# Loading each K or V unit by two 64-partition transfers (even and odd partitions) instead of one

## The chip, the cores and the metric

The kernel runs on one core of one Trainium2 chip. The metric is the device time of one execution in microseconds (us), the median of several. "Unit" is one 512 KB block of the K or V cache, the amount that the kernel loads and consumes at a time.

## The reference

Two rounds of attention over a KV cache (one new token, batch 4, 32 query heads on 8 KV heads, 8192 positions, head size 128) and a gated feed-forward block, each with a layer norm and a residual:

```python
q = (x @ wq).reshape(B, Sq, Hq, Dh) ...            # B=4, Sq=1, D=512, Hq=32, Dh=128
k = jnp.repeat(k_cache, rep, axis=1)               # k_cache, v_cache: (4, 8, 8192, 128) bf16
scores = jnp.einsum("bhqd,bhkd->bhqk", q, k) * (Dh ** -0.5)
o = jnp.einsum("bhqk,bhkd->bhqd", _softmax(scores), v)
...
x = x + A(layernorm(x)); x = x + B(layernorm(x))   # and both once more, same weights and caches
```

Each cache is 67 MB. The kernel keeps 11 of the 32 V units of a batch on chip between the two rounds, so 468 units are loaded: 256 of K and 212 of V, 245 MB, and 14 MB of weights.

## The kernel before

A unit is 2048 cache rows of 256 bytes. Partition p takes rows 16p to 16p+15, a contiguous run of 4 KB. Seven ring slots hold the units in flight; SyncE issues each load as soon as PE has released the slot. `T.dma` adds the waits that are needed and records what the next reader has to wait for.

```python
CR = 2048; NB = CR // P          # P = 128, NB = 16 rows in a partition
NRING = 7
...
def pump():
    while lptr[0] < len(loads):
        kind, x, sm = loads[lptr[0]]
        if kind == "w":                        # a weight piece of 0.9 or 1 MB, every fifth load at first
            T.dma("sp", x[0], x[1], sm, writes=[x[2]])
        else:
            ap, key = home[x]                  # ring slot or kept slot, [128, 2048] bf16
            if not released.get(key, True):
                return
            ...
            src = cache[b, g, c * CR:(c + 1) * CR, :].rearrange("(p t) d -> p (t d)", p=P)
            T.dma("sp", ap, src, sm, writes=[key])
        lptr[0] += 1
```

PE transposes a K unit (16 matmuls), multiplies the transposed unit with the queries, and later multiplies V units with the softmax weights (16 matmuls a unit).

## Time and profile before

698.9 us (median of 3; 697 to 700 us in groups of runs). What matters:

| | before |
|---|---|
| bytes moved by the load queue | 259.3 MB |
| rate in steady stretches | 403 to 409 GB/s |
| transfer time of a unit at 406 GB/s | 1.29 us |
| 468 units and 13.9 MB of weights at that rate | 638 of 700 us |
| one issue on SyncE | 0.33 us |

These lines are from the page of the kernel before: all packets; the load queue with its packets, MB and share of 16 engines' time; the chain of waits that ended last, by engine and by line; the K transposes on PE (count, busy us, mean ns, idle us ahead of them and what ended most of it); and the K loads (count, size, us from issue to landing).

```profile
DMA packets 75117, 260.93 MB, mean 373 GB/s; under 512 B 7672, under 2 KB 13568, under 8 KB 74496
q1 hardware_dynamic: 75008, 259.30, 96.1%
...
PE 51%; DMA 37%; issue 5%; DVE 4%; ACT 2%; SPq 1%; ACTq 0%
...
L408 PE MATMUL ps<-ident,ring 128*128 128x128 bf16 x4096 | 294.6, 230 | 36.8 <-DMA ring<-in_A_k_cache_dram 35.0
...
ring<-in_A_k_cache_dram SPq DMA_DIRECT2D x256, 512.0 KB, 7.6
```

The transfer engines are taken 96% of the time. A K load needs 7.6 us from issue to landing although its own share of the stream is 1.29 us: by these two numbers about five others stand before it.

The windows view of four steady stretches of the kernel before (window and its length in us; busy us of PE, weight load, DVE, ACT and POOL, with counts; granted clock; share of the DMA engines; GB/s):

```profile
100.00:150.00 50.00, 44.83 (x771) 35.14 (x772) 21.54 (x35) 20.03 (x24) 0.00 (x0) 0.88 1.02 403
205.00:245.00 40.00, 38.04 (x618) 29.14 (x615) 25.98 (x46) 22.68 (x29) 0.00 (x0) 0.95 1.02 406
360.00:400.00 40.00, 36.16 (x584) 26.78 (x581) 23.09 (x40) 20.27 (x26) 0.00 (x0) 0.98 1.03 409
520.00:560.00 40.00, 35.99 (x594) 27.08 (x591) 23.41 (x39) 21.38 (x27) 0.00 (x0) 0.98 1.03 409
```

SyncE's own waits in the kernel before (what released it: total us, times, longest us):

```profile
SPq L62 <- PE ps L408: 263.9, 225, 11.8
SPq L62 <- PE ps L507: 157.9, 111, 8.3
```

Its K issues, by source line (count: shortest, median, longest ns; first and last start us):

```profile
L92 SPq DMA_DIRECT2D ring<-in_A_k_cache_dram x256: 327/328/6203, 1.6 to 645.4; - x128
```

And a piece of its timeline (start us, length us; the view joins SyncE's issues of one kind that follow one another, over its pauses too, and counts them behind the x; the eight that take 8.70 us are 0.33 us each, so 6.1 us of that are pauses):

```profile
204.89 1.24 SPq L92 DMA_DIRECT2D ring<-in_A_k_cache_dram  x2
207.13 0.33 SPq L92 DMA_DIRECT2D ring<-in_A_v_cache_dram  x1
208.47 8.70 SPq L92 DMA_DIRECT2D ring<-in_A_k_cache_dram  x8
218.17 0.33 SPq L92 DMA_DIRECT2D ring<-in_A_v_cache_dram  x1
```

### The profile page before, as it was taken

How to read it: one execution, taken by the hardware profiler on the slowest of the kernel's cores; microseconds unless marked ns; L12 is line 12 of the kernel's file. 1: busy time of each engine (PE TensorE's matmuls, PEld its weight loads, DVE VectorE, ACT ScalarE, POOL GpSimd, SP SyncE). 2: the span in 40 equal slices, each digit the busy share in tenths (PEclk: the TensorE clock that was granted, in tenths of full speed). 3: DMA queues.
4: the chain of work that ended last, by engine and by line, in shares of the span. 5: the costliest groups of instructions: out<-in, count | busy, mean ns of one | idle time of the engine just before them, and what ended most of it. 6: DMA issues, size and time to landing. Idle time of an engine off the chain costs nothing.

```text
span 699.7 us, 25539 instructions
## 1 busy us (share of the span) xinstructions
PE 584.9 (84%) x11552; PEld 479.2 (68%) x11552; DVE 298.8 (43%) x635; ACT 235.1 (34%) x296; POOL 0.7 (0%) x6
## 2 busy tenths in 40 slices
PE   3977879878699899987799898988799876799876
PEld 2755657657677687766677677767777675777665
DVE  1544524443156645452165534543155510266501
ACT  1533324331056434420154434432055500055400
POOL 0000000000000000000000000000000000000000
PEclk9999879995589889985599879995589955599855
DMA  8999999999889999999999999999899989999992
GB/s 349 388 388 408 385 395 407 401 401 409 328 284 411 404 399 407 406 408 392 335 343 409 402 370 385 370 409 407 320 382 409 408 325 410 349 338 361 343 396 75
DMA packets 75117, 260.93 MB, mean 373 GB/s; under 512 B 7672, under 2 KB 13568, under 8 KB 74496
## 3 DMA queue, kind: packets, MB, share of 16 engines
q1 hardware_dynamic: 75008, 259.30, 96.1%
q8 instruction: 90, 1.47, 0.9%
q14 instruction: 19, 0.16, 0.1%
HBM read 259.26 MB, written 0.00 MB: 371 GB/s over the span
## 4 chain that ended last, share of the span: by engine, by line
PE 51%; DMA 37%; issue 5%; DVE 4%; ACT 2%; SPq 1%; ACTq 0%
DMA ring<-in_A_k_cache_dram 27%; PE ps L408 25%; PE ps L507 9%; DMA ring<-in_A_v_cache_dram 8%; PE ps L424 7%; PE ps L572 3%; PE ps L596 2%; DMA wq_sb<-in_A_wq_dram 2%; PE ps L531 1%; SPq L92 1%; PE ps L632 1%; PE ps L548 1%; ACT ktp L248 1%; PE ps L479 1%; DVE negm L436 1%
## 5 line engine op out<-in xcount | busy, mean ns | idle before, releaser
L408 PE MATMUL ps<-ident,ring 128*128 128x128 bf16 x4096 | 294.6, 230 | 36.8 <-DMA ring<-in_A_k_cache_dram 35.0
L408 PEld LDWEIGHTS ps<-ident,ring 128*128 128x128 bf16 x4096 | 251.4, 103 | 79.0 <-DMA ring<-in_A_k_cache_dram 54.1
L246 DVE COPY ktp<-ps 128x1024 bf16<-128x1024 bf16 x320 | 215.6, 689 | 206.3 <-PE ps L408 205.4
L248 ACT ACTIVATE ktp<-ps 128x1024 bf16<-128x1024 bf16 x192 | 195.5, 1023 | 259.7 <-PE ps L408 259.7
L424 PE MATMUL ps<-ktp,qpad 128*32 128x512 bf16 x1024 | 111.3, 401 | 3.3 <-ACT ktp L248 2.6
L507 PE MATMUL ps<-pp,ring 128*128 128x4 bf16 x2688 | 88.9, 166 | 22.5 <-issue 13.1
L507 PEld LDWEIGHTS ps<-pp,ring 128*128 128x128 bf16 x2688 | 82.5, 102 | 35.5 <-issue 21.8
L424 PEld LDWEIGHTS ps<-ktp,qpad 128*32 128x32 bf16 x1024 | 27.7, 93 | 37.7 <-ACT ktp L248 7.5
L507 PE MATMUL ps<-pp,kept 128*128 128x4 bf16 x1408 | 45.8, 166 | 8.7 <-DMA kept<-in_A_v_cache_dram 6.3
L507 PEld LDWEIGHTS ps<-pp,kept 128*128 128x128 bf16 x1408 | 41.4, 101 | 16.6 <-DMA kept<-in_A_v_cache_dram 7.9
L564 ACT ACTIVATE lnv<-var,eps_sb 128x4 f32<-128x4 f32 x10 | 3.0, 297 | 142.9 <-DVE var L551 142.9
L515 DVE TENSOR_TENSOR oT<-ps,invL 128x4 bf16<-128x4 f32 x64 | 10.6, 166 | 79.8 <-PE ps L507 79.7
L438 ACT ACTIVATE pp<-ps,negm 128x512 bf16<-128x512 f32 x32 | 22.0, 687 | 26.7 <-DVE negm L436 22.7
L572 PE MATMUL ps<-xnT,wq_sb 128*128 128x4 bf16 x640 | 18.7, 166 | 11.5 <-DMA wq_sb<-in_A_wq_dram 7.7
L436 DVE TENSOR_REDUCE negm<-ps 128x1 f32<-128x512 f32 x32 | 22.1, 690 | 11.6 <-PE ps L424 10.0
L572 PEld LDWEIGHTS ps<-xnT,wq_sb 128*128 128x128 bf16 x640 | 17.9, 104 | 12.0 <-DMA wq_sb<-in_A_wq_dram 7.8
L531 PE MATMUL ps<-oT,wo_sb 128*128 128x4 bf16 x640 | 21.3, 166 | 5.5 <-DVE oT L515 2.9
L531 PEld LDWEIGHTS ps<-oT,wo_sb 128*128 128x128 bf16 x640 | 20.0, 104 | 7.8 <-issue 4.7
L479 PE MATMUL ps<-ident,pp 128*128 128x128 bf16 x128 | 14.5, 303 | 1.3 <-DVE pp L469 1.0
L551 DVE TENSOR_REDUCE var<-ps 128x4 f32<-128x16 f32 x10 | 1.7, 175 | 28.2 <-PE ps L548 28.2
L479 PEld LDWEIGHTS ps<-ident,pp 128*128 128x128 bf16 x128 | 12.4, 140 | 1.9 <-DVE pp L469 1.7
L248 ACT ACTIVATE pp<-ps 128x1024 bf16<-128x1024 bf16 x6 | 6.1, 1025 | 16.8 <-PE ps L479 16.8
(66 smaller groups left out, 158.1 us busy)
## 6 DMA issues: line engine op xcount, KB each, us to landing
ring<-in_A_k_cache_dram SPq DMA_DIRECT2D x256, 512.0 KB, 7.6
ring<-in_A_v_cache_dram SPq DMA_DIRECT2D x168, 512.0 KB, 7.6
kept<-in_A_v_cache_dram SPq DMA_DIRECT2D x44, 512.0 KB, 12.2
wq_sb<-in_A_wq_dram SPq DMA_DIRECT2D x1, 4096.0 KB, 12.4
wo_sb<-in_A_wo_dram SPq DMA_DIRECT2D x4, 1024.0 KB, 11.6
wg_sb<-in_B_w_gate_dram SPq DMA_DIRECT2D x2, 896.0 KB, 12.0
wu_sb<-in_B_w_up_dram SPq DMA_DIRECT2D x2, 896.0 KB, 11.9
wd_sb<-in_B_w_down_dram SPq DMA_DIRECT2D x2, 896.0 KB, 9.2
```

The costliest lines, as they stand in the source:

```text
L246: T.op("dve", lambda e: e.tensor_copy(dst, src), reads=reads, writes=writes)
L248: T.op("act", lambda e: e.activation(dst, src, ACTF.Copy), reads=reads, writes=writes)
L408: T.op("pe", lambda e: e.matmul(stg[:, t * P:(t + 1) * P], lhsT=ap[:, blk * Dh:(blk + 1) * Dh], rhs=ident[:], is_transpose=True, start=Tru ...
L424: T.op("pe", lambda e: e.matmul(ps[32 * j:32 * (j + 1), bk * BW:(bk + 1) * BW], lhsT=qp, rhs=ktp[:, s, (j % 2) * 512:(j % 2 + 1) * 512], s ...
L436: T.op("dve", lambda e: e.tensor_reduce(negm[:, q, c:c + 1], bank(bk), AX.X, ALU.max, negate=True), reads=[f"pb{bk}"], writes=[f"negm{q}_{ ...
L438: T.op("act", lambda e: e.activation(pp[:, q, c * 512:(c + 1) * 512], bank(bk), ACTF.Exp, bias=negm[:, q, c:c + 1], scale=1.0, accum_out=l ...
L479: T.op("pe", lambda e: e.matmul(stg[:, t * P:(t + 1) * P], lhsT=pp[:, q, blk * P:(blk + 1) * P], rhs=ident[:], is_transpose=True, start=Tr ...
L507: T.op("pe", lambda e: e.matmul(ps[:, bk * BW:bk * BW + REP], lhsT=ap[:, (NM * j + m) * Dh:(NM * j + m + 1) * Dh], rhs=pp[:, q, col:col + ...
L515: T.op("dve", lambda e: e.tensor_tensor(oT[:, l, g * REP:(g + 1) * REP, b], ps[:, bk * BW:bk * BW + REP], invL[:, q, g * REP:(g + 1) * REP ...
L531: T.op("pe", lambda e: e.matmul(ps[:, OPJ * BW + nq * B:OPJ * BW + (nq + 1) * B], lhsT=wo_sb[:, h, nq * P:(nq + 1) * P], rhs=oT[:, l, h, : ...
L572: T.op("pe", lambda e: e.matmul(misc[:, h * B:(h + 1) * B], lhsT=wq_sb[:, kt, h * Dh:(h + 1) * Dh], rhs=xnT[:, kt * B:(kt + 1) * B], start ...
L596: T.op("pe", lambda e: e.matmul(ps[:, bk * BW + fo * B:bk * BW + (fo + 1) * B], lhsT=w_sb[:, kt, fo * P:(fo + 1) * P], rhs=xnT[:, kt * B:( ...
```

## The change

Each unit is loaded by two transfers of 256 KB, one into the even and one into the odd partitions. Bytes, runs (4 KB), slots and the place of every row stay the same; the reader waits for both.

```diff
+    NSPL = 2
...
-                    src = cache[b, g, c * CR:(c + 1) * CR, :].rearrange("(p t) d -> p (t d)", p=P)
-                    T.dma("sp", ap, src, sm, writes=[key])
+                    src = cache[b, g, c * CR:(c + 1) * CR, :].rearrange("(p i t) d -> i p (t d)", i=NSPL, t=NB)
+                    for i in range(NSPL):
+                        T.dma("sp", ap[bass.ds(i, P // NSPL, step=NSPL), :], src[i], sm, writes=[key] if i == 0 else [])
+                    T.res[key].w = (sm, T.semval[id(sm)])
```

The intent can only be a better spread or finer grain of the transfers; nothing is taken away.

## The prediction

> **What bounds the kernel now.** The transfers. The page's queue part gives the one queue 96.1% of the 16 DMA engines' span, for 259 MB. By windows, steady stretches (100 to 175, 205 to 330, 355 to 400 us) move 400 to 415 GB/s at a DMA share of about 1.0. At 406 GB/s a 512 KB unit takes 1.29 us; 468 units are 604 us and 13.9 MB of weights 34 us: 638 of 700 us. The rest is at the four block boundaries (near 190, 350, 500, 565 us, 164 to 250 GB/s) and the two ends. PE is busy 84% but follows: in the chain of waits K transfers hold 27%, V transfers 8%. SyncE issues a load when PE has let a slot go (264 and 158 us of its waits), with about 6 of 7 ring slots in flight.
>
> The packet records agree: 59904 packets of 4 KB, median 159 ns, 629.8 us summed over 16 engines; 7672 semaphore packets of 4 bytes, 9.3 ns each.
>
> **What the change does.** Same bytes, same 4 KB packets, same slots and waits. A unit becomes two transfers of 64 partitions (every other one): 468 more transfers.
> - Removed: nothing. The unit's wait is for both.
> - SyncE: an issue is busy 0.33 us; two in a row start 0.37 to 0.43 us apart. Some 0.8 us a unit is under 1.29 us: off the critical path.
> - Engines: one more semaphore packet per engine and unit, 9.3 ns; the first data packet behind one often takes 165 to 172 instead of 159 ns, so 9 to 16 ns each, 4.4 to 7.5 us for 468. About 90% of the span is transfer-bound: 4 to 7 us show.
>
> **The doubtful term: which engine writes which partitions.** [...] only 4 to 7 us are lost: about 704 us. [...] No trace here shows which; I give the first a little over one half. The engines are not in step now (a transfer's 16 landings spread over 2.4 us, median)[...].
>
> **Prediction.** 712 us, between the two; range 698 to 940. Faster by over 2%: 0.03; within 2%: 0.51; slower: 0.46.
>
> **What would show it.** Queue part: about 7490 more packets, all tiny, same MB. If 4 KB packets stay at 159 to 163 ns and steady stretches at 395 to 410 GB/s, the first reading holds: 700 to 710 us. [...] If instead the share falls and SyncE's issues run back to back, issuing limits.
>
> **What would make it wrong.** [...] a costlier transfer boundary than 16 ns; rows 8 KB apart reading slower from HBM than neighbours; a queue that fills sooner with 10 packets per engine and unit instead of 9 (issues blocked up to 6.2 us already occur).

The forecast of 712 us lies between two cases: 704 us, the first reading, which is the kernel before and 4 to 7 us for the boundaries, and a much slower one, which also sets the upper end of the range, 940 us.

## More of the kernel before

The order of rows within a unit does not matter as long as K and V share it; some experiments use that.

SyncE waits 422 of 700 us for PE to release a slot.

SPq, which is SyncE issuing transfers, has 1% of the chain.

## The result, and the profile after

730.2 us (median of 4, 727.4 to 732.7) against 698.8 us: ratio 1.0445, 95% interval 1.038 to 1.051. A ratio here is the mean time of one kernel's fast runs over that of the other's of the same rounds, so not quite the ratio of the medians. The result is correct and 4.5% slower. The time lay inside the range, but the forecast of 712 us had 13 of the 31 us that were lost.

The same lines of the page of the kernel after:

```profile
DMA packets 82609, 260.99 MB, mean 360 GB/s; under 512 B 15160, under 2 KB 21056, under 8 KB 81984
q1 hardware_dynamic: 82496, 259.33, 95.8%
...
PE 39%; DMA 27%; SPq 23%; issue 6%; DVE 3%; ACT 2%; ACTq 0%
...
L411 PE MATMUL ps<-ident,ring 128*128 128x128 bf16 x4096 | 298.3, 231 | 50.7 <-DMA ring<-in_A_k_cache_dram 49.1
...
ring<-in_A_k_cache_dram SPq DMA_DIRECT2D x512, 256.0 KB, 5.4
```

The packets grew by 7488, all of them tiny, as expected. SPq went from 1% to 23% of the chain. A load now lands 5.4 us after its issue instead of 7.6: the queue ahead of it has become shorter, although the kernel is slower. Where SyncE needs longer for a unit in the runs below, it is the same: over all loads the median from issue to landing is 7.7 us before, 5.2 us after, 5.8 us in e5, and 2.6 us in e2, with transfers of 128 KB.

The same four windows:

```profile
100.00:150.00 50.00, 41.30 (x724) 32.41 (x724) 20.14 (x33) 18.57 (x22) 0.00 (x0) 0.88 1.02 391
205.00:245.00 40.00, 37.08 (x576) 27.47 (x572) 24.21 (x37) 22.80 (x26) 0.00 (x0) 1.00 1.01 369
360.00:400.00 40.00, 37.42 (x588) 28.69 (x585) 22.23 (x34) 20.04 (x25) 0.00 (x0) 0.95 0.99 370
520.00:560.00 40.00, 34.16 (x510) 26.45 (x507) 18.95 (x29) 17.93 (x20) 0.00 (x0) 0.88 1.01 378
```

The rate fell from 403 to 409 GB/s to 369 to 391, while the DMA share still reads about 1.0. The share adds up the times of packets, and these grew: the 4 KB packets take 647.8 us of each engine instead of 629.8. In the records of single packets, the median of the 4 KB packets is 159 ns before and after, and those of at most 160 ns even rose from 67 to 88% of all; but those over 250 ns rose from 1.9 to 3.5% (36.6 to 69.0 us of each engine). That these include waiting is the author's reading, not shown. A share of 0.99 to 1.02, as here at 369 to 391 GB/s, is no proof that the engines are the limit.

SyncE in the kernel after, in the same three views, its waits first:

```profile
SPq L62 <- PE ps L411: 37.4, 44, 8.5
...
SPq L62 <- PE ps L510: 15.5, 15, 4.8
```

Its K issues:

```profile
L92 SPq DMA_DIRECT2D ring<-in_A_k_cache_dram x512: 471/596/2760, 1.6 to 670.4; - x171
```

And its timeline from 226 to 236 us:

```profile
226.10 10.16 SPq L92 DMA_DIRECT2D ring<-in_A_k_cache_dram  x15
```

SyncE's waits for PE went from 422 to 53 us. The 15 issues of this timeline take 10.16 us; in their single records the pauses are 0.04 us between the halves of a unit and about 0.10 us around the wait, so SyncE issues nearly without a pause. One issue of 64 partitions takes 0.47 us after a pause and 0.54 to 0.60 us back to back, against 0.33 us (0.38 back to back) for 128 partitions. The shortest cycle of a unit is 0.54 + 0.04 + 0.60 us and about 0.10 us around the wait: 1.28 us, the same as the 1.29 us that the transfers need. In addition 83 of the 936 issues took over 0.75 us (81 in the repeat e14). Had they taken 0.57 us like the others, the mean below would be about 1.27 us (an estimate from these records): it is they that lift it over 1.29. The packet records tell what they go with: 81 of the 83 overlap one of the 90 packets of 16 KB of the page's instruction queue (q8), and 73 end 0.35 to 0.40 us after the end of such a packet, as none of the other 853 issues does. Meeting a packet is not enough: in e5, below, 77 short issues overlap one, and only 5 of 468 issues are long. Why issues hang there is not shown. To have one number for all runs: SyncE's own time per unit is the time from its first to its last cache issue, less its waits for PE and the weight issues, divided by 468. It is 0.54 us before (where 54 of the 468 issues took over 0.75 us, up to 6.2) and (706.8 - 52.9 - 6.3) / 468 = 1.38 us after.

Theory 1: SyncE's issuing limits the changed kernel. Theory 2, the rival: the 468 additional transfer boundaries cost the 16 engines, 31 us / 468 = 67 ns each.

### The profile page after: what moved, and what is told of

The parts are those of the page before. It is cut to its first block, busy times and chain, and to the rows that moved or that the text cites. A ratio compares the mean times of both kernels' runs of the same rounds, so it can differ in the third digit from the quotient of the medians.

```text
span 725.5 us, 26007 instructions
## 1 busy us (share of the span) xinstructions
PE 592.1 (82%) x11552; PEld 483.5 (67%) x11552; DVE 299.5 (41%) x635; ACT 235.1 (32%) x296; POOL 0.7 (0%) x6
## 4 chain that ended last, share of the span: by engine, by line
PE 39%; DMA 27%; SPq 23%; issue 6%; DVE 3%; ACT 2%; ACTq 0%
SPq L92 23%; PE ps L411 20%; DMA ring<-in_A_k_cache_dram 19%; DMA ring<-in_A_v_cache_dram 6%; PE ps L427 5%; PE ps L510 5%; PE ps L575 2%; DMA wq_sb<-in_A_wq_dram 2%; PE ps L599 2%; ACT ktp L249 1%; PE ps L534 1%; DVE negm L439 1%; PE ps L635 1%; PE ps L551 1%; DMA kept<-in_A_v_cache_dram 1%
## 5 line engine op out<-in xcount | busy, mean ns | idle before, releaser
L411 PE MATMUL ps<-ident,ring 128*128 128x128 bf16 x4096 | 298.3, 231 | 50.7 <-DMA ring<-in_A_k_cache_dram 49.1
L411 PEld LDWEIGHTS ps<-ident,ring 128*128 128x128 bf16 x4096 | 254.8, 104 | 93.9 <-DMA ring<-in_A_k_cache_dram 67.3
L510 PE MATMUL ps<-pp,ring 128*128 128x4 bf16 x2688 | 90.6, 166 | 28.8 <-DMA ring<-in_A_v_cache_dram 15.9
```

Of the source, the lines that this page charges most:

```text
L411: T.op("pe", lambda e: e.matmul(stg[:, t * P:(t + 1) * P], lhsT=ap[:, blk * Dh:(blk + 1) * Dh], rhs=ident[:], is_transpose=True, start=Tru ...
L510: T.op("pe", lambda e: e.matmul(ps[:, bk * BW:bk * BW + REP], lhsT=ap[:, (NM * j + m) * Dh:(NM * j + m + 1) * Dh], rhs=pp[:, q, col:col + ...
```

## The experiments

Seventeen runs, all with correct results. Each diff is against the kernel before, unless said.

### e1, e5, e6, e15: SyncE delayed, transfers untouched

```diff
+                    T.wait_res("sp", writes=[key])
+                    for _ in range(18):                # e5 and e15: 30, e6: 48
+                        nc.sync.wait_ge(sem_x, 16)     # satisfied since the start
                     T.dma("sp", ap, src, sm, writes=[key])
```

e1, 

> The kernel before (one transfer of 128 partitions per unit), with 18 waits on an already satisfied constant put in front of each unit's issue on SyncE, some 0.9 us, so that SyncE needs about 1.3 us per unit as in the changed kernel. Transfers, packets and layout are those of before. Theory 1, SyncE's issuing limits the changed kernel (two issues of 0.54 and 0.60 us plus the wait are 1.28 us a unit, and 1.29 us is what the transfer engines need): slower than before by 3 to 7%, 720 to 748 us, SyncE's waits for PE nearly gone. Theory 2, the extra transfer boundaries on the 16 engines cost (31 us over 468 more transfers are 67 ns each): no extra transfers here, so within 1% of before, 695 to 706 us.

Measured: 701.1 us, ratio 1.006 (0.999 to 1.013). This lies in theory 2's range, but the dose was too small: the waits were fused in pairs, SyncE's own time was 1.02 us a unit, and it still waited 201 us for PE. So neither theory is tested by it, but it sets a lower bound: 1.02 us a unit cost next to nothing.

e5, 

> As e1_slow_issue, with more delay. In e1 the waits were fused in pairs, 9 instructions of 0.06 us, so a unit needed only 0.97 us of SyncE (the smallest distance of two issues) and SyncE still waited 219 us: that dose was under the 1.29 us of the transfers. Here 30 waits are 15 instructions, 0.91 us on top of 0.43: 1.34 us a unit with one transfer of 128 partitions. Theory 1 (SyncE's issuing limits the changed kernel): 715 to 740 us. Theory 2 (the extra transfer boundaries cost): within 1.5% of before, 690 to 709 us.

Measured: 720.5 us, ratio 1.0295 (1.025 to 1.034). With not one additional transfer, most of the loss is there. SyncE's own time was 1.40 us a unit. The windows of e5, same columns as above:

```profile
100.00:150.00 50.00, 43.94 (x723) 34.43 (x724) 20.06 (x32) 18.61 (x22) 0.00 (x0) 0.80 1.00 381
205.00:245.00 40.00, 37.97 (x592) 28.21 (x589) 24.58 (x37) 23.42 (x27) 0.00 (x0) 1.00 0.99 374
360.00:400.00 40.00, 37.47 (x622) 28.38 (x619) 24.05 (x37) 21.45 (x25) 0.00 (x0) 1.00 0.97 369
```

The rate is that of the changed kernel, with a DMA share of 0.97 to 1.00, and the packets over 250 ns take 61 us of each engine, against 69.0 in the changed kernel and 36.6 before: in e5 they came with slow feeding alone, without the split.

e6, 

> The same with 48 waits, 24 instructions, 1.45 us on top of 0.43: 1.88 us a unit. Theory 1: 468 units of 1.88 us are 881 us, with start and end 895 to 930 us, and the 4 KB packets stay at a median of 159 ns. Theory 2: as before, 690 to 709 us.

Measured: 944.0 us (one look, so its state is unknown), 14 us over theory 1's range. SyncE's own time was 1.95 us a unit. In two steady windows (300 to 340 and 500 to 540 us) the stream moved 267 and 270 GB/s, and still showed a DMA share of 0.82 and 0.83. So somewhere between 1.02 us (e1) and 1.40 us (e5) a unit SyncE's time begins to count, and at 1.95 us it sets the time.

e15, 

> e5 once more: SyncE at 1.4 us a unit with single transfers. If all of the change's loss were SyncE's time per unit, it would lie within 3 us of e14. If the gap of e5 is real, it is 718 to 723 us, 7 to 11 us under e14.

Measured: 723.4 us, ratio 1.035 (1.031 to 1.039), on one chip with e14 (below); at the edge of its range, and 6.6 us under e14 by the means, where 7 to 11 were expected.

### e2: four transfers of 32 partitions

```diff
-    NSPL = 2          # against the kernel after
+    NSPL = 4
```

> The changed kernel with four transfers of 32 partitions per unit (every fourth partition) instead of two. Theory 1: if an issue keeps its 0.54 to 0.60 us, a unit needs about 2.4 us of SyncE, 468 units 1120 us, so 1100 to 1200 us; 4 KB packets stay at a median of 159 ns. Theory 2: three extra boundaries a unit at 67 ns each are 94 us: 780 to 800 us.

Measured: 1285.3 us. Theory 2 would have 780 to 800. It lies over theory 1's range because an issue of 32 partitions costs as much as one of 64 (median 0.594 us against 0.596), but now always the back-to-back price. SyncE's own time was 2.70 us a unit, its waits for PE 1 us. Its K issues:

```profile
L92 SPq DMA_DIRECT2D ring<-in_A_k_cache_dram x1024: 468/594/1977, 1.6 to 1202.6; - x171
```

The expectation of untouched packets was half a miss: the median stayed at 159 ns, but 24% of the 4 KB packets took over 250 ns, in a stream of 198 and 201 GB/s (300 to 340 and 500 to 540 us). (In e6, with untouched transfers, 10% did, so at least a part of this goes with a starved stream.)

### e3, e8, e16, e17: SyncE relieved

In e3 GpSimd, which is idle (0.7 us busy in the kernel before), issues the odd half of every unit, with a semaphore of its own; PE waits for both.

```diff
+                    src = ...  "(p i t) d -> i p (t d)"
+                    T.dma("sp", ap[bass.ds(0, P // 2, step=2), :], src[0], sm, writes=[key])
+                    T.dma("pool", ap[bass.ds(1, P // 2, step=2), :], src[1], sem_odd[key], writes=[key + "o"])
```

> The changed kernel, but the odd partitions' transfer of each unit is issued by GpSimd, which is idle, with a semaphore of its own; same number of transfers, same partitions, same 4 KB packets. Theory 1: SyncE issues one transfer a unit (about 0.5 us) and is no longer the limit; if GpSimd needs under 1.2 us for its half, the time goes back to 698 to 712 us. Theory 2: the boundaries are the same, so it stays at 725 to 735 us. If GpSimd's own issuing takes more than 1.3 us a transfer, it is slower than both and tells nothing.

Measured: 730.5 us, ratio 1.048 (1.039 to 1.056). By its time alone theory 1 would have fallen. The trace says more: SyncE waited 407 us for PE again, and its later steady slices moved up to 411 GB/s. PE's progress through the units shows where the time went: e3 was 13 us behind the kernel before at its 128th unit (the changed kernel only 4.5 us), and while the next 160 units passed it lost 3.5 us more (the changed kernel 8.8). The early loss falls where the weight pieces of 1 MB stand in SyncE's queue only, and 34 of the 39 units whose halves landed over 3 us apart lie in the first 101 us. So e3 added a new trouble and was repeated without it: in e8 GpSimd takes the odd halves only of loads after the last weight piece.

> As e3_pool_half, but GpSimd takes the odd halves only of the loads after the last weight piece; before that both halves come from SyncE as in the changed kernel. In e3 SyncE waited for PE 425 us again and the steady stretches moved 400 to 411 GB/s, but 13 of its 28 us were lost by the 128th unit, while the 1 MB weight pieces stood in SyncE's queue alone and the two halves of a unit came apart. Theory 1: 700 to 714 us, and 4 KB packets and steady stretches as before. Theory 2: the same boundaries as in the changed kernel, 725 to 735 us.

Measured: 716.0 us, ratio 1.024 (1.019 to 1.029): between the two theories and a miss of both ranges. SyncE's waits and the four windows of e8:

```profile
SPq L62 <- PE ps L415: 205.8, 205, 8.3
SPq L62 <- PE ps L514: 156.2, 99, 12.5
```

```profile
100.00:150.00 50.00, 41.08 (x726) 32.11 (x727) 20.04 (x33) 18.61 (x22) 20.13 (x38) 0.90 1.01 389
205.00:245.00 40.00, 37.66 (x593) 28.04 (x593) 25.23 (x40) 23.49 (x28) 16.09 (x30) 1.00 1.02 401
360.00:400.00 40.00, 38.39 (x626) 29.03 (x623) 23.41 (x36) 21.87 (x27) 17.18 (x32) 1.00 1.03 408
520.00:560.00 40.00, 37.47 (x624) 28.63 (x621) 23.02 (x36) 22.17 (x26) 17.05 (x32) 1.00 1.03 410
```

In the last two windows the same 64-partition transfers run at 408 and 410 GB/s, as fast as the single transfers before (409). That refutes 67 ns a boundary. In the first two they do not quite (389 and 401 against 403 and 406). About half of the loss stayed, which e16 and e17 ask about.

```diff
+            T.wait_res("pe", reads=[key])              # e16: at the start of each unit
+            nc.tensor.wait_ge(sem_x, 16)               # satisfied since the start
```

> The kernel before with one more wait of PE at the start of every unit, on a semaphore long satisfied: what the second semaphore of e3 and e8 costs. If it explains what e8 has left, 705 to 712 us; if not, 698 to 702 us.

Measured: 704.2 us, ratio 1.0095 (1.005 to 1.014): between the two ranges, so a miss of both. One more satisfied wait of PE per unit costs some 0.5 to 1.4%; its trace does not show where, because the profiled execution (701.5 us) was no slower than that of the kernel before. That e3 and e8 pay as much for the second semaphore that PE waits on there is argued from this, not shown.

> e8_pool_late with the source of each half contiguous, as in e13. If the 6.5 us of the source stride are real and do not depend on SyncE being the limit, 706 to 712 us (ratio about 1.014, of which the second semaphore of PE is 0.0095). If the stride counts only where SyncE limits, as e8, 713 to 719 us.

Measured: 712.8 us, ratio 1.020 (1.015 to 1.025). That is between the two; its interval overlaps that of e8. A part of what e8 has left is the change itself: SyncE issues both halves of its first 54 units, and at the 54th PE was already 3.4 us behind the kernel before (the profiled executions; the changed kernel 1.6, so the sizes are rough). The rest is not explained by these runs.

### e4, e11, e12: what a boundary costs when SyncE has slack

e4 and e12 are the same kernel: two transfers of all 128 partitions, each of half the columns (2 KB runs). e11 moves the same 2 KB packets by one transfer.

```diff
+                    HC = NB * Dh // NSPL                # e4, e12
+                    for i in range(NSPL):
+                        T.dma("sp", ap[:, i * HC:(i + 1) * HC], src[:, i * HC:(i + 1) * HC], sm, writes=[key] if i == 0 else [])
```

```diff
+                    src = cache[...].rearrange("(a p t) d -> p a (t d)", a=NSPL, p=P)      # e11
+                    T.dma("sp", ap.rearrange("p (a x) -> p a x", a=NSPL), src, sm, writes=[key])
```

> Each unit in two transfers of all 128 partitions, each of half the columns (2 KB runs), both issued by SyncE. It shows the price of an issue when the number of partitions is 128 and not 64: if it is 0.33 to 0.40 us as before, SyncE is at 0.85 us a unit and waits for PE again; if it is 0.54 to 0.60 us, the price belongs to a run that is not the whole contiguous block. The 2 KB packets, worked out from 159 ns for 4 KB and 46 to 48 ns for 1 KB, take about 84 ns, 16 of them 1.34 us a unit against 1.27 us: 468 units are 33 us longer, so 730 to 745 us in either case; the verdict is read from SyncE's issue durations and waits.

Measured: 722.9 us, 7 us under the stated range; ratio 1.036 (1.030 to 1.043). The K issues of e4:

```profile
L92 SPq DMA_DIRECT2D ring<-in_A_k_cache_dram x512: 327/432/4197, 1.6 to 665.9; - x171
```

An issue of 128 partitions takes 0.33 to 0.43 us, also when its runs are pieces of a row. SyncE's own time was 1.12 us a unit and it waited 172 us for PE, so it was not the limit; the loss is the 2 KB packets (median 85 ns, so 16 of them 1.36 us a unit), as e11 confirms, which has them without the split.

> One transfer of 128 partitions a unit, but with two runs of 2 KB in each partition (rows are dealt to partitions in two groups of 8, the same for K and V, so the result is right). The same packets as e4_columns and half its transfers; SyncE has slack in both, so the difference to e4/e12 is what 468 more transfer boundaries cost the engines. My prediction had 9 to 16 ns each: 715 to 719 us here against 723 us, 4 to 8 us. Theory 2 at 67 ns each: 692 to 697 us here, 31 us under e4.

> e4_columns once more, beside e11 on the same chip: 719 to 727 us.

Measured on one chip: e11 722.8 us, e12 723.3 us. The means differ by 0.2 us, 95% interval (Student's t, six runs each) plus or minus 2.2 us. So 468 more transfers on the engines cost at most about 2.4 us, 5 ns each. Theory 2 falls, and with it the term of 4 to 7 us in my prediction; e11 missed its range of 715 to 719 us accordingly. The two also differ in their source: the runs of one transfer of e12 lie 4 KB apart, those of e11 side by side. So here, where SyncE has slack, distance shows no cost either.

### e7: halves of neighbouring partitions

```diff
+                    src = ... "(i p t) d -> i p (t d)"
+                    for i in range(NSPL):
+                        T.dma("sp", ap[bass.ds(i * (P // NSPL), P // NSPL), :], src[i], sm, writes=[key] if i == 0 else [])
```

> Two transfers a unit, of the partitions 0 to 63 and 64 to 127, each from one contiguous half of the unit's 512 KB. Is the dearer issue (0.54 and 0.60 us, against 0.33 and 0.38 us for 128 partitions, and 0.38 to 0.43 us in e4_columns) a matter of the step of two, or of 64 partitions? If of the step, issues are 0.33 to 0.43 us and SyncE waits for PE again. If of the number of partitions, issues stay at 0.47 to 0.60 us and SyncE limits, 720 us or more. [...]

Measured: 1028.7 us (median of the three fast runs; two slow ones took 1051.7 and 1086.6), ratio 1.48 (1.465 to 1.490). The profiled execution of e7 was the slowest one, so only its issues, packets and SyncE's waits are used, roughly:

```profile
L92 SPq DMA_DIRECT2D ring<-in_A_k_cache_dram x512: 465/596/8255, 1.6 to 1005.7; - x171
```

Issues cost the same with neighbouring partitions and contiguous sources as with a step of two (median 0.596 us in both): here the price goes with 64 partitions, not with the step. And the 4 KB packets took 275 ns (median) instead of 159. SyncE waited 402 us for PE, so issuing at 1.40 us a unit was not the limit; the longer packets go with the loss. Why neighbouring partitions lengthen them is not shown. With even and odd partitions the packets kept 159 ns, and the stream reached 410 GB/s (e8).

### e9, e10: half the dose

```diff
+                    for i in range(NSPL if x[0] == "v" else 0):     # e10: "k"
+                        T.dma(... the two transfers of the change ...)
+                    if x[0] != "v":
+                        T.dma("sp", ap, ... the one transfer of before ...)
```

> Only V units are loaded by two transfers (212 of the 468 units), K units by one as before. Theory 1 (SyncE's issuing limits, a threshold): where K and V units alternate, a unit needs about (0.45 + 1.33) / 2 = 0.9 us of SyncE, under the 1.29 us of the transfers, so nearly nothing is lost: 698 to 707 us, SyncE's waits for PE over 150 us. Theory 2 (each extra boundary costs 67 ns on the engines, additive): 212 of 468 of 31 us, 14 us: 711 to 717 us. Together with e10: theory 1 has the two losses sum to well under the 31 us of the whole change, theory 2 to about 31 us.

> Only K units are loaded by two transfers (256 of the 468 units), V units by one. Theory 1: 699 to 710 us, a little more than e9 because K units come in longer rows. Theory 2: 256 of 468 of 31 us, 17 us: 713 to 720 us.

Measured: e9 711.1 us, ratio 1.014 (1.010 to 1.018); e10 708.9 us, ratio 1.011 (1.008 to 1.015). e9 missed theory 1's range by 4 us and lies at the lower edge of theory 2's; e10 lies in theory 1's. The two losses sum to 2.5%, where the whole change loses 4.5%: less than additive, as a threshold has it, but not nothing. SyncE's own time is 0.92 and 1.04 us on average and it waits 255 and 196 us, but the average hides stretches of one kind, in which SyncE may still limit. That is argued, not shown: in the last 32 units, V alone, e9 lost 2.9 us against the kernel before, but the changed kernel, which splits them too, lost 1.4 there, and e10, which does not, 1.3.

### e13, e14: the rest of the gap

e14 is the kernel after once more. e13 keeps its stepped partitions, but each half reads one contiguous 256 KB:

```diff
-                    src = ... "(p i t) d -> i p (t d)"      # against the kernel after
+                    src = ... "(i p t) d -> i p (t d)"
```

> The changed kernel with the same stepped partitions, but each transfer reads one contiguous 256 KB half of the unit (rows are dealt to partitions otherwise, the same for K and V, so the result is right). If source rows 8 KB apart cost anything, this is faster than e14 by 4 us or more; if not, it is within 3 us of e14, and SyncE's issues stay at 0.47 to 0.60 us.

> The changed kernel once more, beside e15: 726 to 734 us, ratio 1.04 to 1.05.

Measured on one chip with e15: e14 728.9 us, ratio 1.045 (1.040 to 1.050); e13 721.7 us, 1.036 (1.031 to 1.040); e15, the delayed single transfers, 723.4 us, 1.035. By the means e13 is 6.5 us (plus or minus 4.6) and e15 6.6 us (plus or minus 4.3) faster than e14, and they agree with each other. So of the 4.5% issuing makes 3.0 to 3.5, and source rows 8 KB apart about 1, which this one comparison shows. SyncE's own time is 1.38 and 1.39 us in e14 and e13. How the distance of the rows works, the trace does not show: packets are alike, and only the median from issue to landing fell from 5.2 to 4.9 us; and e13's profiled execution was its slowest. e17 against e8 did not show the same gain clearly, nor e11 against e12; on what the gain depends is not shown.

| run | transfers a unit, partitions | SyncE's own us a unit | SyncE waits for PE, us | median us | ratio |
|---|---|---|---|---|---|
| before | 1 of 128 | 0.54 | 422 | 698.8 | |
| e1 | 1 of 128, delayed | 1.02 | 201 | 701.1 | 1.006 |
| e4 | 2 of 128, 2 KB runs | 1.12 | 172 | 722.9 | 1.036 |
| after, e14 | 2 of 64 | 1.38 | 53 | 730.2, 728.9 | 1.045 |
| e13 | 2 of 64, source contiguous | 1.39 | 49 | 721.7 | 1.036 |
| e5, e15 | 1 of 128, delayed | 1.40 | 43 | 720.5, 723.4 | 1.030, 1.035 |
| e6 | 1 of 128, delayed | 1.95 | 5 | 944.0 | (one look) |
| e2 | 4 of 32 | 2.70 | 1 | 1285.3 | 1.841 |

No run beat the kernel before, and none of the findings points to a version that would.

## Why the prediction was right or wrong

- "The transfers" bound the kernel before: right. Delayed by 0.5 us a unit (e1) it did not move clearly (701.1 us); delayed to 1.40 and 1.95 us a unit (e5, e6), over the 1.29 us of the transfers, it took 720.5 and 944.0 us.
- "Same 4 KB packets, 7490 more tiny ones": right, 7488.
- "Which engine writes which partitions": the first reading held. With even and odd partitions the packets kept 159 ns (median); with neighbouring halves (e7) they took 275. The 712 us were a mixture of 704 us and a slower case, with longer packets, that did not occur. The upper end of the range, 940 us, stood for the same case, so that 730 us lies inside the range is luck.
- "SyncE: an issue is busy 0.33 us; two in a row start 0.37 to 0.43 us apart. Some 0.8 us a unit is under 1.29 us: off the critical path." This is the step that failed. The durations were read rightly, but from transfers of 128 partitions. An issue of 64 partitions takes 0.47 to 0.60 us, so the unit needs 1.28 us at best and 1.38 us on average, over the 1.29 us of the transfers, where 0.8 was forecast. Some 0.11 us of the 1.38 are the 83 long issues, most of which end with a packet of the instruction queue; why stays open. e5 and e15 show the effect by itself: 3.0 to 3.5% of the 4.5%.
- "9 to 16 ns each, 4.4 to 7.5 us for 468": too dear. e11 and e12 have it at 0.2 us, plus or minus 2.2. The 165 to 172 ns of the packet behind a semaphore packet are not special to it either: in the kernel before, 18% of the 6159 packets of 4 KB that start 3 ns before a semaphore packet ends took that long, and 16% of all others.
- "Rows 8 KB apart reading slower from HBM than neighbours" stood among the things that could go wrong, with no size. e13 and e14 show 6.5 us, plus or minus 4.6.
- "If instead the share falls and SyncE's issues run back to back, issuing limits": the issues do run back to back, but the share did not fall. The sign was wrong in that half: in the four windows the rate falls from 403 to 409 GB/s to 369 to 391, the share stays at 0.99 to 1.02.

## What to carry to other kernels

The price of an issue is to be measured for the shape that will be issued: here an issue of half the partitions (0.47 to 0.60 us) was dearer than one of all (0.33, 0.38 to 0.43 back to back), and two of them, 1.38 us a unit on average, outgrew the 1.29 us of the transfer itself. Before transfers are split, compare the issuing engine's time per unit, waits taken out, with the transfer's time per unit. When the DMA share reads 1.0, look at the rate, at the time from issue to landing and at the issuer's waits as well: here K loads landed after 5.4 us instead of 7.6 and SyncE's waits for PE fell from 422 to 53 us while the kernel got 4.5% slower, so the queue was starved, not full.
